# Attention and mixture of experts on one core: the experts' order moved behind the first expert's row numbers, and the low half of w2 taken last in the early tiles

## Chip, cores and metric

The kernel runs on one core of one Trainium2 chip. The metric is the device time of one execution in microseconds (us), as the median over several runs. Engine names are those of the profile: PE is TensorE, PEld its weight loads, DVE is VectorE, ACT is ScalarE, POOL is GpSimd and SP is SyncE.

## What is computed

A linear attention without softmax runs over 8 batches, 8 heads, 576 positions and head dimension 64. Its rows, normalized and scaled, are the 4608 tokens of 512 features of a mixture of 8 experts with one expert per token:

```python
kv = np.einsum('bhsd,bhse->bhde', k, v)
out = np.einsum('bhsd,bhde->bhse', q, kv)
x = out / np.sqrt(np.mean(out * out, axis=-1, keepdims=True) + 1e-06) * g_norm   # as [4608, 512]
...
expert_idx = np.argmax(x @ w_gate, axis=1)         # gate_w: the softmax value of that expert
...                                                # each expert keeps its first 1152 tokens
h = np.maximum(np.einsum('ecd,edf->ecf', disp, w1), 0.0)   # 512 -> 1024
y = np.einsum('ecf,efd->ecd', h, w2)                       # 1024 -> 512
out[i] = gate_w[i] * y[expert_idx[i], pos[i]]
```

## The kernel before

The work has two stages, and each stage's order is written by a planner (class `Plan`). An operation names its engine with an assumed duration, the operations that it depends on, and a key. The planner goes forward in time: of all that is ready it takes what can start first, and the lower key among equals. Each engine then executes its instructions in the order that came out, waiting in order for what is not there yet. A table of small shifts of keys by operation number (`NUDGE`) belongs to each of the two plans.

The first plan runs the attention, batch by batch. `route` finds each token's expert, its place in that expert's list, and enters the token's number into a table in PSUM (`enter`, line 1046), which needs three one-hot products on DVE (`ohh`, `ohl`, `rhs`). It also writes the rows to `x_dram`. Beside it, one expert is chosen early from the tokens of the first batches (`pick`), its two weight matrices are loaded and split into a high and a low half of 16 bits (`high`, `low`, lines 393 to 405), and its first 384 rows go through both products at the end of the plan (`early_products`): three tiles of 128 rows, of which the second product of tile 0 belongs to the first plan and those of tiles 1 and 2 to the second.

Each second product of a tile of 128 rows sums 24 matmuls into one PSUM bank: three blocks of 8, which are the high half of the hidden rows by the high half of w2, the high half by the low half of w2, and the low half of the hidden rows by the high half of w2 (`Gemm2.terms`). The planner issues them in groups of 4 (`second`), and each group depends on those pieces of the hidden rows and of w2 that it reads.

`finish` (line 1343) stands between the stages. It reads the finished table (`read_table`), works out the row numbers of the rest of the first expert's rows (`cut`, whose last instruction writes `gi_rest`, line 1154), the row numbers of all experts (`sources`, line 1145), where results are written (`cut2`, with `targets`), the tokens per expert (`count`, whose result is copied at line 1088), and the order of the other seven experts from that count (`rank_steps`, lines 1108 to 1137: compare, rank, turn and keep, the last of which writes `perm_i`). All of that is on DVE, except for one matmul of the count.

The second plan runs the experts one after the other (`products`). For the first, the remaining 320 rows are gathered by `gi_rest` (POOL, line 457), multiplied by their norm (DVE, line 465), transposed on PE and cast on ACT. For the next expert, POOL copies its number into `next_i` (line 1762) behind those three gathers, SP reads it and starts the loads of w1 (line 345); DVE reads the expert's column of `perm_i` into a register and copies its row numbers (`slots`, lines 668 and 673); POOL gathers its rows, which are transposed by DMA (line 501). Line 713 is a helper of copies and casts, line 551 the first product, line 597 the second, and line 361 the maximum over a piece of weights.

Of the kernel before, what the change touches and what calls it, by code (L numbers as in the profile page):

```python
# [20 lines left out]
EARLY = 384  # L21
# [168 lines left out]
def attention_moe_kernel(  # L190
# [12 lines left out]
    nc = tc.nc  # L203
# [9 lines left out]
    KF = F // P  # L213
# [7 lines left out]
    ep = ctx.enter_context(tc.tile_pool(name="ep", bufs=1))  # L221
# [95 lines left out]
    wsets = [[wts.tile([P, KD * F], F16, name=f"w{n}_0") for n in ("1h", "1l", "2h", "2l")]]  # L317
# [255 lines left out]
    class Gemm2:  # L573


        def __init__(self, pool, ws, g, gt, sidx, s0, s1, bufs=3):
            self.pool, self.g, self.gt, self.sidx, self.s0, self.bufs = pool, g, gt, sidx, s0, bufs
            self.w = [w.rearrange("p (j d) -> p j d", j=KF) for w in ws[2:4]]
            self.tiles = spans(s0, s1)
            self.ysc = pool.tile([P, NHI], F32, name="ysc")  # L580
            hh, hl = g.hh, g.hl
            self.terms = [(h, w, j) for h, w in ((hh, self.w[0]), (hh, self.w[1]), (hl, self.w[0])) for j in range(KF)]

        def scales(self, scale):
            c0 = 0
# [119 lines left out]
    op = plan.op  # L705
# [374 lines left out]
        writes.append(ws)  # L1080
        lasts[b] = ws + [ent, acc]

    def count(dst, key):

        cp = misc[:, 64:64 + E]
        o = op(("T", 0.05), lambda e: nc.tensor.matmul(cp, lhsT=ones16, rhs=tot_acc, start=True, stop=True), accs[-1:], FIRST)
        readers.setdefault("acc", []).append(o)
        return op(("V", 0.1), lambda e: nc.vector.tensor_copy(dst, cp), [o], key)

    def distinct(cnt):  # L1090
        d = sm.tile([P, E], F32, name="dist")
# [72 lines left out]
    early = {}  # L1164
# [97 lines left out]
    def second(r, st, hh, hl, w2, scaled, hid, w_hold, sl_hold, s0, s1, bank, tiles=range(NHI), key=None):  # L1262

        key = KEY * r if key is None else key
        urgent = key - KEY
        for i, (_, m, _) in enumerate(spans(s0, s1)):
            if i not in tiles:
                continue
            yp, o = new(bank[0]), None
            k = key + 5 + 0.1 * i  # L1270
            if m > NARROW:
                for c in range(0, 3 * KF, 4):

                    def product(e, i=i, c=c, yp=yp):
                        if c == 0:
                            yp.t = bank[1]()
                        st["g2"].products(i, yp.t, c, c + 4)

                    js = range(c % KF, c % KF + 4)
                    after = [(hl if c >= 2 * KF else hh)[j] for j in js] + [scaled, o]  # L1280
                    after += [w2[KF <= c < 2 * KF][j] for j in js] if w2 else []
                    o = op(("T", 0.86), product, after, k, (yp,), (hid, w_hold))
            else:
                yt = new("ysb")

                def product(e, i=i, yp=yp):
                    yp.t = bank[1]()
                    st["g2"].turned_products(i, yp.t)

                o = op(("T", 0.1 + TURNED_PAIR[m] if m <= PAIRED else m / 25 + 0.25), product, hh + hl + [scaled] + [x[j] for x in w2 or () for j in range(KF)], k, (yp,),  # L1290
                       (hid, w_hold))
                o = op(("V", 0.07 + (8 if m <= PAIRED else 4) * m / 960), lambda e, i=i, yp=yp: st["g2"].keep(i, yp.t), [o], urgent, (yt,), (yp,))
                yp = new(bank[0])

                def turn(e, i=i, yp=yp):
                    yp.t = bank[1]()
                    st["g2"].turn(i, yp.t)

                o = op(("T", 0.4), turn, [o], key + KEY + 0.05, (yp,), (yt,))
            yh = new("ysb")  # L1300

            def out_(e, i=i, yp=yp, yh=yh):
                yh.t = st["g2"].out(i, yp.t)

            o = op(("A", 0.58), out_, [o], urgent, (yh,), (yp,))
            o = op(("P", 1.05), lambda e, i=i, yh=yh: st["g2"].write(i, yh.t), [o], key, (), (yh, sl_hold))
            o = op(("D", 0.73), None, [o], key, (), (yh,))
        return o

    def early_products():  # L1310
        st = early["st"] = {}
        gates, xh, xl = early["turns"]
        early["hh"], early["hl"] = hh, hl = [], []
        for j in range(KF):
            nm = "x" if j < ON_X else "op"
            hp = new(nm)
            o = None
            for t in range(3):

                def products(e, j=j, t=t, hp=hp, nm=nm):  # L1320
                    if "g1" not in st:
                        st["g1"] = Gemm1(ep, wsets[0], early["x"]().xs, EARLY, EARLY)
                        st["g1"].hidden()
                    hp.t = hp.t or bank(nm)
                    st["g1"].products(j, hp.t, (t,))

                ws = [early["w", 0][t == 2][2 * c + j // (KF // 2)] for c in range(KD)]
                o = op(("T", 4 * EARLY / 2400 + 0.02), products, (xl if t == 1 else xh) + ws + [o], LOW, (hp,))
            a = op(("A", 0.05 + EARLY / 1200), lambda e, j=j, hp=hp: st["g1"].high(j, hp.t), [o], LOW, (), (hp,))
            hh.append(a)  # L1330
            hl.append(op(("V", 0.07 + EARLY / 960), lambda e, j=j, hp=hp: st["g1"].low(j, hp.t), [a], LOW, (), (hp,)))

        def scales(e):
            st["g2"] = Gemm2(ep, wsets[0], st["g1"], early["x"]().gt, early["si"], 0, EARLY, 2)
            st["g2"].scales(y_scale(*[early["z", i]["e"] for i in range(2)]))

        early["scaled"] = op(("V", 1.2), scales, gates + hh[:1] + list(early["w", 1][0].values()), LOW)
        second(-1, st, hh, hl, early["w", 1], early["scaled"], Hold(None), Hold(None), Hold(None), 0, EARLY,
               ("op", lambda: bank("op")), range(EARLY_TILES), LOW + 2)

    cnt_all = cst.tile([P, E], F32, name="cnt_all")

    def finish():
        key = NB * C
        t = op(("V", 0.45), lambda e: read_table(), enters[-1:] + early["slots"] + early["slots2"], key)

        def cut(e):
            early["gi0"] = ep.tile([P, NHI], I32, name="gi_rest")
            sources_of_first(early["gi0"])

        def cut2(e):
            targets()
            early["si0"], = slots(ep, early["first"], ("si",), EARLY)

        early["cut"] = op(("V", 0.65), cut, [t], key)
        early["sources"] = op(("V", 0.2), lambda e: sources(), [t], key + 0.1)
        early["cut2"] = op(("V", 0.8), cut2, [t], key + 0.3)
        o = count(cnt_all, key)
        for long, f in rank_steps(cnt_all):
            o = op(("V", long), lambda e, f=f: f(), [o], key + 0.2)  # L1360
        early["rank"] = o

    tiles = {0: load(0)}
# [446 lines left out]
```

## Time and profile before

| what | us |
|---|---|
| median of 3 runs | 559.38 |
| lowest and highest of them | 556.1 and 563.11 |
| the profiled execution | 556.98 |
| its span, first to last instruction | 555.1 |
| PE busy | 520.3 |
| DVE busy | 394.1 |
| ACT busy | 252.7 |
| POOL busy | 150.9 |

The profiled execution is one run of its own. The span lies 1.9 us under its time, for what stands ahead of the first and behind the last instruction. Its mean granted PE clock is 0.985 of 2.4 GHz. Times within the profile are counted from the first instruction. The attention stage reaches to about 155 us, the experts from there to 548.

### The profile page before, as it was taken

The numbers are of one execution on the slowest core, as the hardware profiler recorded it, in microseconds if no ns is written. First come the engines' busy times: TensorE is split into PE (matmuls) and PEld (weight loads), VectorE is DVE, ScalarE is ACT, GpSimd is POOL, SyncE is SP. The second block draws the span as 40 slices with busy tenths as digits, with TensorE's granted clock in tenths as the row PEclk, the third lists the DMA queues.
The fourth block names the chain that finished last, engine by engine and source line by source line (L and its number), as shares of the span: only waits on it lengthen the run. The fifth ranks groups of instructions, "written<-read, shape, count | busy, mean of one in ns | idle before, by whom it ended". The sixth has DMA issues, their size and how long they took to land.

```text
span 555.1 us, 12017 instructions
## 1 busy us (share of the span) xinstructions
PE 520.3 (94%) x4599; PEld 344.2 (62%) x4599; DVE 394.1 (71%) x1041; ACT 252.7 (46%) x506; POOL 150.9 (27%) x173
## 2 busy tenths in 40 slices
PE   4989797898996999999999999999999999999995
PEld 4878695876544666546754675667468648745442
DVE  3389679989967679869868899779778785751200
ACT  1667475698413346237246282264246165212210
POOL 6001002612356553243404320220503151002011
PEclk9999798899999999999999999999999999999998
DMA  8999999744256979778619538747529341001010
GB/s 272 358 356 360 392 380 368 252 144 182 98 155 249 226 242 264 154 151 266 159 49 322 144 92 280 139 144 259 142 65 305 115 119 38 1 20 58 0 40 32
DMA packets 78019, 102.58 MB, mean 185 GB/s; under 512 B 43222, under 2 KB 51414, under 8 KB 76932
## 3 DMA queue, kind: packets, MB, share of 16 engines
q1 hardware_dynamic: 69600, 70.43, 43.3%
q0 software_dynamic: 7776, 31.30, 16.0%
q8 instruction: 38, 0.62, 0.5%
q14 instruction: 25, 0.20, 0.1%
q10 hardware_dynamic: 580, 0.02, 0.1%
HBM read 73.13 MB, written 20.61 MB: 169 GB/s over the span
## 4 chain that ended last, share of the span: by engine, by line
PE 19%; issue 18%; DMA 11%; DVE 3%; POOL 1%; ACT 1%; POOLq 0%; DVEq 0%
DMA out_dram<-ysb,si 11%; PE hp L551 11%; PE yp L597 6%; DVE am L361 2%; PE yp L612 1%; ACT w2h L395 1%; POOL xg L457 1%; DVE hb L559 1%; POOL out_dram L637 0%; POOL gt L472 0%; POOLq L1740 0%; POOLq L637 0%; DVE xm L465 0%; ACT hb L556 0%; DVE w2l L401 0%
## 5 line engine op out<-in xcount | busy, mean ns | idle before, releaser
L551 PE MATMUL hp<-xs,w1h 128*128 128x320 f16 (+6 forms) x896 | 134.6, 300 | 5.7 <-ACT xs L713 2.6
L597 PEld LDWEIGHTS <-hb 128*128 128x128 f16 x840 | 81.2, 98 | 93.4 <-issue 0.7
L597 PE MATMUL yp<-w2h,hb 128*128 128x512 f16 x544 | 127.1, 379 | 0.3 <-ACT ysb L632 0.2
L551 PEld LDWEIGHTS <-w1h 128*128 128x128 f16 x960 | 93.3, 98 | 46.9 <-issue 7.8
L637 POOL DMA_INDIRECT out_dram<-ysb,si x41 | 46.3, 1130 | 238.1 <-ACT ysb L632 180.8
L361 DVE TENSOR_REDUCE am<-raw 128x1 f32<-128x512 f32 x120 | 75.3, 677 | 12.5 <-DMA raw<-in_moe_w_dram 12.4
L556 ACT ACTIVATE hb<-hp 128x320 f16<-128x320 f32 (+7 forms) x64 | 40.6, 636 | 84.8 <-PE hp L551 70.9
L559 DVE SCALAR_TENSOR_TENSOR hb<-hp,hb 128x320 f16<-128x320 f32 (+7 forms) x64 | 47.2, 737 | 35.8 <-ACT hb L556 35.6
L551 PE MATMUL hp<-xs,w1l 128*128 128x320 f16 (+6 forms) x448 | 71.5, 300 | 0.0
L632 ACT ACTIVATE ysb<-yp,ysc 128x512 f32<-128x512 f32 (+5 forms) x40 | 27.4, 684 | 94.2 <-PE yp L597 90.9
L597 PE MATMUL yp<-w2l,hb 128*128 128x512 f16 x272 | 64.7, 379 | 0.0
L551 PEld LDWEIGHTS <-w1l 128*128 128x128 f16 x480 | 46.9, 98 | 19.4
L457 POOL DMA_INDIRECT xg<-x_dram,gi x35 | 37.1, 1061 | 34.5 <-DVE xm L465 19.8
L861 PE MATMUL op<-kv_bd,qt 128*128 128x144 f32 x256 | 44.2, 316 | 1.6 <-ACT qt L713 1.1
L401 DVE SCALAR_TENSOR_TENSOR w2l<-raw,sw,w2h 128x512 f16<-128x512 f32 x64 | 44.8, 743 | 0.5 <-ACT w2h L395 0.4
L401 DVE SCALAR_TENSOR_TENSOR w1l<-raw,sg,w1h 128x512 f16<-128x512 f32 x64 | 45.0, 746 | 0.0
L491 ACT CAST pair<-xm 128x512 f16<-128x512 f32 (+5 forms) x35 | 21.3, 615 | 46.1 <-DVE xm L465 24.1
L395 ACT ACTIVATE w1h<-raw,sg 128x512 f16<-128x512 f32 x60 | 38.8, 711 | 7.0 <-DVE sg L390 7.0
L395 ACT ACTIVATE w2h<-raw,sw 128x512 f16<-128x512 f32 x62 | 40.1, 713 | 1.0 <-DVE sw L331 1.0
L861 PEld LDWEIGHTS op<-kv_bd,qt 128*128 128x128 f32 x256 | 37.8, 210 | 3.8 <-ACT qt L713 1.8
L772 PE MATMUL a<-v_sb,k_sb 64*64 64x64 f32 x576 | 23.6, 233 | 9.2 <-DMA v_sb<-in_v_dram 7.4
L772 PEld LDWEIGHTS a<-v_sb,k_sb 64*64 64x64 f32 x576 | 20.7, 145 | 12.9 <-issue 11.6
(250 smaller groups left out, 634.6 us busy)
## 6 DMA issues: line engine op xcount, KB each, us to landing
raw<-in_moe_w_dram SPq DMA_DIRECT2D x64, 512.0 KB
k_sb<-in_k_dram SPq DMA_DIRECT2D x16, 576.0 KB
v_sb<-in_v_dram SPq DMA_DIRECT2D x16, 576.0 KB
x_dram<-o_sb POOLq DMA_DIRECT2D x8, 1152.0 KB
q_sb<-in_q_dram SPq DMA_DIRECT2D x16, 512.0 KB
x_dram<-o_sb POOLq DMA_DIRECT2D x8, 144.0 KB
q_sb<-in_q_dram SPq DMA_DIRECT2D x32, 32.0 KB
out_dram<-ysb,si POOLq DMA_INDIRECT x41
```

What stands on the lines that cost most here:

```text
L361: nc.vector.tensor_reduce(out=am()[:, p:p + 1], in_=raw[:, sl(p)], axis=AX.X, op=ALU.max, apply_absolute_value=True)
L395: nc.scalar.activation(wh[:, sl(p)], raw[:, sl(p)], AF.Copy, scale=z["s"])
L401: nc.vector.scalar_tensor_tensor(out=wl[:, sl(p)], in0=raw[:, sl(p)], scalar=z["s"], in1=wh[:, sl(p)], op0=ALU.mult, op1=ALU.subtract)
L457: nc.gpsimd.indirect_dma_start(out=self.xg[i][0:n], out_offset=None, in_=x_dram[0:self.rows, :], in_offset=bass.IndirectOffsetOnAxis(ap=se ...
L551: nc.tensor.matmul(self.view(hp)[:, u], lhsT=w[:, c, j * P:(j + 1) * P], rhs=x[:, c, u * hw:(u + 1) * hw], start=(t == 0 and c == 0), stop ...
L556: nc.scalar.activation(self.out(self.hh, j), self.view(hp), AF.Relu)
L559: nc.vector.scalar_tensor_tensor(out=self.out(self.hl, j), in0=self.view(hp), scalar=0.0, in1=self.out(self.hh, j), op0=ALU.max, op1=ALU.s ...
L597: nc.tensor.matmul(yp[0:n, 0:DM], lhsT=h[:, j, o:o + n], rhs=w[:, j, :], start=(m == 0), stop=(m == len(self.terms) - 1))
L632: nc.scalar.activation(self.ysb[0:n], yp[0:n, 0:DM], AF.Copy, scale=self.ysc[0:n, i:i + 1])
L637: nc.gpsimd.indirect_dma_start(out=out[:, :], out_offset=bass.IndirectOffsetOnAxis(ap=self.sidx[0:n, col:col + 1], axis=0), in_=ysb[0:n], ...
L772: nc.tensor.matmul(banks[g].t[rows[u], half * D:(half + 1) * D], lhsT=kh.t[rows[g], u, c * D:(c + 1) * D], rhs=vh.t[rows[g], u, c * D:(c + ...
L861: nc.tensor.matmul(y, lhsT=qt.t[:, i * P:(i + 1) * P], rhs=kv2[:, half * HH + i], start=True, stop=True)
```

## The change

Two things are changed. In `finish`, the copy of the count and the four pieces of the experts' order get a dependency on `cut`, so the planner can't place them ahead of the first expert's row numbers. In the early tiles (those of the first 384 rows), the second product's three blocks are summed in another order: high by high, low of the hidden rows by high of w2, and then high by low of w2. The dependencies of the groups follow that order. The other tiles keep theirs. Number and form of the instructions, and the numbering of the operations, stay as they were.

```diff
-        def __init__(self, pool, ws, g, gt, sidx, s0, s1, bufs=3):
+        def __init__(self, pool, ws, g, gt, sidx, s0, s1, bufs=3, low_last=False):
...
-            self.terms = [(h, w, j) for h, w in ((hh, self.w[0]), (hh, self.w[1]), (hl, self.w[0])) for j in range(KF)]
+            pairs = [(hh, self.w[0]), (hh, self.w[1]), (hl, self.w[0])]
+            self.terms = [(h, w, j) for h, w in (pairs[::2] + pairs[1:2] if low_last else pairs) for j in range(KF)]
...
-    def count(dst, key):
+    def count(dst, key, behind=None):
...
-        return op(("V", 0.1), lambda e: nc.vector.tensor_copy(dst, cp), [o], key)
+        return op(("V", 0.1), lambda e: nc.vector.tensor_copy(dst, cp), [o, behind], key)
...
-                    after = [(hl if c >= 2 * KF else hh)[j] for j in js] + [scaled, o]
-                    after += [w2[KF <= c < 2 * KF][j] for j in js] if w2 else []
+                    block = (0, 2, 1)[c // KF] if r < 0 else c // KF
+                    after = [(hl if block == 2 else hh)[j] for j in js] + [scaled, o]
+                    after += [w2[block == 1][j] for j in js] if w2 else []
...
-            st["g2"] = Gemm2(ep, wsets[0], st["g1"], early["x"]().gt, early["si"], 0, EARLY, 2)
+            st["g2"] = Gemm2(ep, wsets[0], st["g1"], early["x"]().gt, early["si"], 0, EARLY, 2, True)
...
-        o = count(cnt_all, key)
+        o = count(cnt_all, key, early["cut"])
         for long, f in rank_steps(cnt_all):
-            o = op(("V", long), lambda e, f=f: f(), [o], key + 0.2)
+            o = op(("V", long), lambda e, f=f: f(), [o, early["cut"]], key + 0.2)
```

## Rows read from the trace of the kernel before

**Rows 1.** The page, busy time, share of the span and instructions of each engine

```profile
PE 520.3 (94%) x4599; PEld 344.2 (62%) x4599; DVE 394.1 (71%) x1041; ACT 252.7 (46%) x506; POOL 150.9 (27%) x173
```

**Rows 2.** Windows: length; busy PE, PEld, DVE, ACT, POOL; PEclk; DMA share; GB/s

```profile
94.30:101.10 6.80, 6.50 (x36) 5.72 (x37) 5.91 (x30) 3.93 (x9) 3.91 (x4) 0.50 0.98 371
160.00:170.00 10.00, 7.98 (x43) 3.94 (x41) 4.97 (x13) 1.54 (x3) 7.12 (x9) 1.00 0.84 257
...
180.00:190.00 10.00, 10.00 (x65) 6.05 (x63) 7.01 (x14) 2.88 (x6) 5.62 (x7) 1.00 0.91 225
```

**Rows 3.** Timeline of PE: start, us, line, op, out<-in, count, idle before<-releaser

```profile
91.88 0.71 PE L1046 MATMUL tab<-rhs,ohl 128*128 128x96 f16 x5 [2.49 <-DVE rhs L1039]
...
153.32 1.89 PE L597 MATMUL op<-w2h,hb 128*128 128x512 f16 x8
155.05 0.71 PE L1046 MATMUL tab<-rhs,ohl 128*128 128x96 f16 x5
155.99 3.61 PE L597 MATMUL yp<-w2h,hb 128*128 128x512 f16 x16 [0.23 <-ACT ysb L632]
...
166.94 1.04 PE L597 MATMUL yp<-w2h,hb 128*128 128x512 f16 x4
170.53 2.08 PE L551 MATMUL hp<-xs,w1h 128*128 128x320 f16 x12 [2.56 <-ACT xs L713]
...
174.98 1.25 PE L551 MATMUL hp<-xs,w1h 128*128 128x320 f16 x8 [0.74 <-DVE am L361]
...
177.69 1.25 PE L551 MATMUL hp<-xs,w1h 128*128 128x320 f16 x8 [0.91 <-DVE hb L559]
...
199.69 1.16 PE L551 MATMUL hp<-xs,w1h 128*128 128x336 f16 x7 [0.16 <-DMA xs<-pair]
```

**Rows 4.** Timeline of ACT

```profile
169.62 0.86 ACT L713 CAST xs<-xp 128x512 f16<-128x512 f32 x2 [5.24 <-remote]
```

**Rows 5.** Timeline of POOL

```profile
156.23 1.07 POOL L637 DMA_INDIRECT out_dram<-ysb,si  x1 [5.61 <-DVE tab_sb L1141]
158.15 1.03 POOL L457 DMA_INDIRECT xg<-x_dram,gi_rest  x1 [0.86 <-issue]
...
161.69 0.18 POOL L1762 COPY next_i<-perm_i 1x1 int32<-1x1 int32 x1
...
169.68 1.06 POOL L465 TENSOR_TENSOR xm<-xg 128x512 f32<-128x512 f32 x1 [1.19 <-remote]
```

**Rows 6.** Timeline of DVE, the next expert's w1

```profile
173.25 1.28 DVE L361 TENSOR_REDUCE am<-raw 128x1 f32<-128x512 f32 x2 [0.80 <-DMA raw<-in_moe_w_dram]
```

**Rows 7.** Timeline of DVE around the table and the row numbers

```profile
151.92 0.74 DVE L401 SCALAR_TENSOR_TENSOR w2l<-raw,sw,w2h 128x512 f16<-128x512 f32 x1
...
152.95 0.16 DVE L1088 COPY cnt_all<-misc 128x8 f32<-128x8 f32 x1
...
153.17 0.16 DVE L1092 SCALAR_TENSOR_TENSOR dist<-cnt_all,desc 128x8 f32<-128x8 f32 x1
...
153.71 0.30 DVE L1035 TENSOR_TENSOR ohh<-cols,col 128x240 f16<-128x240 f16 x1
...
154.40 0.45 DVE L1039 TENSOR_TENSOR rhs<-ohh,tok_hl 128x480 f16<-128x480 f16 x1
...
155.80 0.21 DVE L1141 TENSOR_SCALAR tab_sb<-tab 128x48 f32<-128x48 f32 x1
...
156.16 0.16 DVE L1133 CAST perm_i<-perm 128x8 int32<-128x8 f32 x1
...
156.34 0.23 DVE L1150 TENSOR_TENSOR mine<-tab_sb,first 128x48 f32<-128x48 f32 x1
...
156.84 0.44 DVE L1154 TENSOR_SCALAR gi_rest<-mine_g 128x6 int32<-128x6 f32 x1
...
157.92 0.17 DVE L673 COPY gi<-gidx_tab 128x6 int32 x1 [0.58 <-DVE tw L1159]
...
161.70 0.71 DVE L465 TENSOR_TENSOR xm<-xg 128x512 f32<-128x512 f32 x1
```

## The prediction

> **What bounds the kernel now.** I read the page's busy shares first, then the windows of 10 us, then the timelines of the engines around the place of the change. The shares say TensorE: 520.3 of a span of 555.1 us [rows 1]. An average over stages with different limits is not enough, so the windows come next. The change sits at about 150 us, where the attention stage hands over to the expert stage. Ahead of it nothing can move, since the planner places work forward in time and the first changed dependency belongs to work at about 150 us. Behind it the windows show a TensorE that is full: 10.00 of 10 us at 180 to 190 [rows 2], and the same in most windows up to 540. The one exception of size is 160 to 170, with 7.98 of 10 [rows 2]. So a gain can only come from TensorE's idle time from 150 us on, and a loss only from new idle time there.
>
> The timeline of TensorE names those gaps. I count 0.23 us at 155.99, 2.56 at 170.53, 0.74 at 174.98, 0.91 at 177.69 and 0.16 at 199.69 [rows 3], together 4.60 us. That is the most that the change can give back there, 0.8% of the run. Faster by over 2% would take 11 us. I did not use the page's chain of waits: behind its end it runs over the write queue of GpSimd, which TensorE does not wait for.
>
> Who ends the gaps? The first product of the rest of the first expert (170.53) waits for the casts of the transposed rows. ScalarE made two of them from 169.62 on, after 5.24 us of idling, released by something that the profile calls remote [rows 4]. The rows that they cast had been transposed by 166.94 [rows 3], and GpSimd's first norm of the next expert began at 169.68 out of the same kind of wait [rows 5]. So most of the 2.56 us is not the row numbers arriving late; two engines were let go together by one late event. The gap at 174.98 is VectorE's: it held a maximum of the next expert's w1 until the load landed (0.80 us, start 173.25), with the low half that frees the product's bank queued behind it [rows 6].
>
> **Part one: the order behind the row numbers.** It adds no instruction, only moves some on VectorE. Before, the work in front of the first expert's row numbers includes the count's copy (the first of three small instructions between 152.95 and 153.17, so 0.07 us) and the comparison (from 153.17 until 153.71, 0.54 us); both stand ahead of the one-hot products, whose last, rhs, starts at 154.40 and takes 0.45 [rows 7]. Then come three rank pieces, run while TensorE enters the last rows in the table, until the table is read at 155.80 (155.80 - 154.85, some 1.0 us), then the rank's keep (156.16 to 156.34, 0.18 us), and then the cut, whose last instruction writes gi_rest from 156.84 on in 0.44 us [rows 7]. The end is 157.28.
>
> After it, copy, comparison and keep stand behind the cut. The one-hot products come 0.07 + 0.54 = 0.61 us sooner, and the cut another 0.18 sooner. The 1.0 us of rank pieces bring the cut nothing: they were covered by the entering on TensorE. The upper bound is 0.61 + 0.18 = 0.79 us.
>
> The lower bound comes from TensorE's own queue. Entering started at 155.05, straight behind two groups of four products of early tile 0 that ran from 153.32 [rows 3]. With the groups about 0.86 us apart, the boundary between them is at 154.19, and rhs would now end at about 154.24 (154.40 + 0.45 - 0.61). If the plan puts entering between the groups, nearly all of the 0.61 is had; if it leaves it behind both, none is, and 0.18 us remain. I take the middle, 0.5 us, because the boundary and rhs fall within 0.05 us of each other and nothing decides for either side.
>
> What this moves: the first gather (158.15) and the two behind it, then the small copy next_i at 161.69, which GpSimd runs behind the three gathers [rows 5], and which SyncE needs to start the loads of the next expert's w1. All come 0.5 us sooner. The 0.80 us wait for a w1 load then shrinks by 0.5, and with it the 0.74 us gap of TensorE. The gap at 170.53 stays as it is in this sum, by what was said of it.
>
> One thing can eat the move. gi_rest took 0.44 us while GpSimd issued a row write (from 156.23, 1.07 us), and the first instruction of the table's reading, before that write began, took 0.21 [rows 5, 7]; the two engines seem to hold each other up by some 0.2 us an instruction. Behind the change the rank's small instructions run beside the three gathers, where the slot reads did (157.92 to 161.70). If two or three of them hold a gather up by 0.2 us each, the 0.5 us are gone and the sum is zero. I take nothing off, because the gathers ran beside the slot reads already. The Trainium skill has a rule for this, which speaks against the change: SBUF — State Buffer, in its single rule on the shared port pair, has VectorE in a two-port mode and GpSimd, which writes descriptors, exclude each other for a whole instruction. By that rule the sum would be zero too, and the trace's 0.44 us agrees with it in kind.
>
> **What is queued behind the rank now.** The rank ends later: from the cut's end (156.8) come the sources, the targets and the slots of the first expert, about 1.3 us, an estimate: the four slot reads stand (161.70 - 157.92) / 4 = 0.95 us apart, and a few small instructions come beside one [rows 7]. Then come 0.07 + 0.54 + 1.0 + 0.18 = 1.8 us of rank, so its end is at about 159.9. next_i has its turn on GpSimd at 161.2, so 1.3 us of cover stand between; without them the w1 loads would slip by whatever is over. The next expert's slots (gi at 157.92) need the rank too and go to about 160.8 if they follow at once. If the plan puts the first norm of the gathered rows (161.70) ahead of them, they end at about 161.2 + 0.71 + 0.95 = 162.9, while GpSimd could take that expert's first gather at about 161.5. That is a delay of up to 1.3 us for the rows of the next expert, whose products waited for their last transposed rows by 0.16 us already [rows 3]. Their first norm had to wait until 169.68 for another reason [rows 5], so I cost this at nothing; if that wait is gone, up to 1.3 us can show at 199.
>
> **Part two: the low half of w2 last.** The 24 products of an early tile stay 24, of the same shape. In tile 0 the last low-half instruction on VectorE ended at 152.66 (from 151.92, 0.74 us), and the products that follow those of the low half start at 153.32 with no idle time in front of them [rows 3, 7]. So on the chip there was no stall to remove. Tiles 1 and 2 start at 155.99, long behind all halves. Bounds: zero below (no stall seen), and above it the 0.23 us in front of 155.99, which hangs on tile 0's end; I take zero. The wait that it could add is on the low half of the hidden rows, which is ready before the last of w2's.
>
> **The sum.** 0.5 us off the gap at 174.98, zero elsewhere: the profiled execution took 556.98 us, which gives 556.5. The three timed runs have the median 559.38, 2.4 us above the profiled one, and spread over 7 us. Taken from the median, 558.9 us.
>
> **The rivals.**
> *Hidden anyway, no change.* Entering stays behind both groups, or the gathers lose 0.5 us to the small instructions beside them. For it: entering's place is decided by 0.05 us, and the 0.44 us of gi_rest; against it: keep's 0.18 us come in any case. Time 559.4 (559.2 to 559.6).
> *The gap at 170.53 goes as well.* If the remote wait is a chance of that one execution or moves with the gathers, 2.56 us come off beside the 0.5: 556.3. For it: nothing in the kernel explains the wait; against it: it may be in every run of both kernels, or in none of the timed ones of before.
> *Next expert's rows late.* The slots case above: 1.3 us at 199, less 0.5: 560.2.
> *The clock falls (the other side).* A gap of 2.49 us in front of 91.88 [rows 3] was followed by a stretch of 6.80 us at a granted 0.50, that is 1.2 GHz [rows 2], while the 2.56 us gap at 170.53 was not: the clock stayed at 1.00 there [rows 2]. A longer gap or a later one there, from slipped w1 loads, can bring such a stretch in front of full work. Its price is half of 6.80, 3.4 us: 562.8. It decides once the idle time around 168 to 178 grows past what stands there now (2.56, 0.74, 0.91 us); the distance is small since a gap of 2.49 did it elsewhere. The Trainium skill's page TensorE: Matmul & The Clock Gate, Part 1, says the throttled state is the default and activity lifts it. By that rule an idle stretch that grows brings the price again, and the trace agrees with its two levels.
>
> **How the numbers follow.** Forecast (0.2 to 1.0 us faster) 0.36; no change 0.20; the large gap gone 0.20; rows late 0.10; clock 0.10; 0.04 for an order that the plan shifts in a later, now full stage by more than 11 us, 0.03 of it slower. The measurement can tell some 2% (11 us) from no change, so the chances are faster 0.01, same 0.96, slower 0.03. The range takes in the gap gone, less 1.5 us for the spread of runs of one kernel (554.8), up to the clock case (562.8). The likeliest one's own range is 558.4 to 559.2 beside the same median.
>
> **What would show it.** In the changed profile gi_rest should end at about 156.5 to 157.1, the rank's pieces should stand behind it, and next_i at about 161.2. Entering should stand between two groups of four products if the larger gain is had. The maximum of w1 should wait 0.3 us and not 0.80. The forecast is wrong if TensorE is idle in front of 170 for more than 2.6 us, if a second stretch at 0.50 stands behind 150, if the next expert's first product waits for transposed rows by over 1 us, or if a full window behind 180 is full no more.

## The result and the profile after

The changed kernel takes 565.88 us (median of 20 runs, 560.49 to 569.72), against 560.15 for the kernel before beside it (20 runs, 556.1 to 567.15): a ratio of 1.0093, 95% interval [1.0067, 1.0119]. That is within 2%, but it is slower, 3 us over the upper end of the predicted range, where half a microsecond of gain was forecast.

The profiled execution took 566.58 us, with a span of 564.8 against 555.1. The page of the changed kernel, busy time by engine:

```profile
PE 522.7 (93%) x4599; PEld 345.5 (61%) x4599; DVE 396.6 (70%) x1042; ACT 252.9 (45%) x506; POOL 150.8 (27%) x172
```

The work is the same; PE is busy 2.4 us longer [rows 1] and idle 7.3 us longer. Of the 9.7 us, 2.16 were there before the first changed instruction (`hi_i`, ahead of the one-hot products, began at 155.04 against 152.88, on an order of DVE that is the same until then), so they are a difference between two executions. For the rest, windows of the changed kernel (length; busy PE, PEld, DVE, ACT, POOL; granted clock; DMA share; GB/s):

```profile
150.00:200.00 50.00, 45.65 (x319) 26.62 (x318) 40.34 (x113) 16.45 (x31) 26.63 (x28) 1.00 0.66 200
200.00:210.00 10.00, 4.42 (x21) 2.28 (x20) 6.24 (x14) 4.60 (x8) 6.61 (x5) 0.77 0.50 145
210.00:220.00 10.00, 10.00 (x64) 6.49 (x63) 4.96 (x13) 3.29 (x5) 3.32 (x4) 0.89 0.93 354
200.00:250.00 50.00, 44.42 (x264) 26.41 (x263) 35.95 (x69) 18.04 (x29) 21.26 (x24) 0.93 0.68 195
```

And the same two long windows of the kernel before:

```profile
150.00:200.00 50.00, 45.28 (x313) 25.91 (x312) 36.68 (x104) 16.54 (x31) 27.94 (x32) 1.00 0.72 208
200.00:250.00 50.00, 49.49 (x308) 28.87 (x307) 39.55 (x84) 20.32 (x34) 17.66 (x23) 1.00 0.85 210
```

The stretch of the change, 150 to 200, is no worse than before. The loss stands behind it, between 200 and 250, where PE does 5.1 us less, and where the clock fell: a window of 10 us at 0.77 holds 4.6 us at 0.50, that is 1.2 GHz, and one at 0.89 holds 2.2. The timeline of PE in the changed kernel:

```profile
155.48 1.89 PE L598 MATMUL op<-w2l,hb 128*128 128x512 f16 x8
157.21 0.71 PE L1047 MATMUL tab<-rhs,ohl 128*128 128x96 f16 x5
158.15 5.34 PE L598 MATMUL yp<-w2h,hb 128*128 128x512 f16 x24 [0.23 <-ACT ysb L633]
...
172.70 1.25 PE L551 MATMUL hp<-xs,w1h 128*128 128x320 f16 x8 [2.66 <-ACT xs L714]
174.42 0.70 PE L551 MATMUL hp<-xs,w1h 128*128 128x320 f16 x4 [0.47 <-DVE xs L485]
177.74 1.25 PE L551 MATMUL hp<-xs,w1h 128*128 128x320 f16 x8 [0.99 <-DVE p2t L329]
207.56 4.36 PE L551 MATMUL hp<-xs,w1h 128*128 128x336 f16 x15 [5.58 <-DMA xs<-pair]
```

The gaps up to 180 are 0.23, 2.66, 0.47 and 0.99 us, 4.35 together, where they were 4.44 [rows 3]. The new one is 5.58 us at 207.56: the second expert's first products wait for the last of its rows to be transposed. That wait was 0.16 us [rows 3]. Why the rows are late is on POOL and DVE of the changed kernel:

```profile
194.11 1.16 POOL L495 TENSOR_TENSOR pair<-xm,pair 128x512 f16<-128x512 f32 x1 [1.23 <-ACT pair L491]
195.45 3.93 POOL L638 DMA_INDIRECT out_dram<-ysb,si  x1 [0.18 <-ACT w1h L395]
199.38 2.83 POOL L472 COPY gt<-xg 32x1 f32<-32x1 f32 x1
202.18 1.14 POOL L495 TENSOR_TENSOR pair<-xm,pair 32x512 f16<-32x512 f32 x1
```

```profile
194.19 1.63 DVE L465 TENSOR_TENSOR xm<-xg 32x512 f32<-32x512 f32 x1
195.74 2.72 DVE L401 SCALAR_TENSOR_TENSOR w1l<-raw,sg,w1h 128x512 f16<-128x512 f32 x4
...
199.44 2.72 DVE L401 SCALAR_TENSOR_TENSOR w1l<-raw,sg,w1h 128x512 f16<-128x512 f32 x4
```

A row write that takes POOL 1.07 us elsewhere [rows 5] took 3.93, and a copy of 32 numbers 2.83, both beside four low halves of w1 that DVE ran without a break. The last tile's low half (`pair`, 32 rows) stood behind them on POOL, began at 202.18 and ended at 203.32; its transposed rows let PE go on at 207.56. In the kernel before, on POOL:

```profile
193.73 1.03 POOL L637 DMA_INDIRECT out_dram<-ysb,si  x1 [0.18 <-ACT w1h L395]
196.00 1.18 POOL L495 TENSOR_TENSOR pair<-xm,pair 32x512 f16<-32x512 f32 x1 [1.24 <-ACT pair L491]
```

There it ended at 197.18, which is 199.34 with the 2.16 us between the two executions, so some 4.0 of the 5.58 us are its lateness. The rest stands between its end and PE's start, 4.24 us against 2.51 before (199.69 - 197.18); no run here explains that part.

### The profile page after: what moved, and what is told of

Its sections match the earlier page's. It is cut to its first block, busy times and chain, and to the rows that moved or that the text cites. A ratio compares the mean times of both kernels' runs of the same rounds, so it can differ in the third digit from the quotient of the medians.

```text
span 564.8 us, 12013 instructions
## 1 busy us (share of the span) xinstructions
PE 522.7 (93%) x4599; PEld 345.5 (61%) x4599; DVE 396.6 (70%) x1042; ACT 252.9 (45%) x506; POOL 150.8 (27%) x172
## 4 chain that ended last, share of the span: by engine, by line
PE 40%; issue 17%; DMA 11%; DVE 5%; POOL 2%; ACT 1%; POOLq 0%; DVEq 0%; SPq 0%
PE hp L551 20%; PE yp L598 14%; DMA out_dram<-ysb,si 6%; DMA raw<-in_moe_w_dram 3%; PE op L551 2%; PE yp L613 2%; DMA x_dram<-o_sb 1%; DVE w2l L401 1%; PE op L598 1%; DVE am L361 1%; POOL xg L457 1%; POOL gt L472 1%; DMA xs<-pair 1%; ACT w2h L395 1%; DMA xg<-x_dram,gi_rest 1%
## 5 line engine op out<-in xcount | busy, mean ns | idle before, releaser
L551 PE MATMUL hp<-xs,w1h 128*128 128x320 f16 (+6 forms) x896 | 136.1, 303 | 11.6 <-DMA xs<-pair 5.6
L457 POOL DMA_INDIRECT xg<-x_dram,gi x35 | 35.9, 1025 | 45.2 <-DVE am L361 19.1
```

The costliest lines, as they stand in the source:

```text
L457: nc.gpsimd.indirect_dma_start(out=self.xg[i][0:n], out_offset=None, in_=x_dram[0:self.rows, :], in_offset=bass.IndirectOffsetOnAxis(ap=se ...
L551: nc.tensor.matmul(self.view(hp)[:, u], lhsT=w[:, c, j * P:(j + 1) * P], rhs=x[:, c, u * hw:(u + 1) * hw], start=(t == 0 and c == 0), stop ...
```

## The experiments

The plan of the expert stage starts from where the first plan leaves each engine. Printed from the planner, the change moves the early expert's row numbers 0.55 us sooner there and the experts' order 3.5 us later (145.31 to 148.80 us of the plan's time), and with it the time from which DVE is free (146.96 to 148.80). From those times the second plan came out in another order on every engine. Three theories: **A**, that new order costs the time; **B**, the order of the experts is late on the chip and the next expert waits; **C**, the low half taken last costs it. Ratios are to the kernel before in the same runs, with their 95% intervals.

**One part alone, and the order alone.** The first two runs make one part of the change each; the third keeps both parts but starts the second plan from the due times of the kernel before, so that the expert stage has exactly its old order; the fourth is the kernel before with the due times of the changed one.

```diff
-    plan = Plan(plan.free, NUDGE[1])
+    for n, end in {...}.items():
+        plan.ops[n].end = end
+    plan = Plan({...}, NUDGE[1])
```

> Part one alone (the count and the experts' order behind the row numbers), the products' blocks as before. The planner gives the expert stage the same order as in the changed kernel. Theory A (the loss is the expert stage's new order, which follows from the order's later due time): 1.009 times before, some 565 us, with a TensorE gap of 5 to 6 us in front of the second expert's first product. Theory B (the rank is late on the chip itself): the same, 1.009. Theory C (the low half last does it): 1.000, 560 us, no such gap.

Measured: 1.0076 [1.0036, 1.0115]. In its profile PE is busy for 44.58 us between 200 and 250, as in the changed kernel, but the gap of 5 to 6 us in front of the second expert's first product isn't there: the two longest waits are 2.87 us at 221.64 and 2.55 us at 233.57, both for hidden rows. So the loss comes with this order, and the place of the gap doesn't.

> Part two alone (the block with the low half of w2 last), the rank as before. Theory C: 1.009 times before with the gap of 5 to 6 us. Theories A and B: the gap in front of the second expert's first product is not that of the changed kernel. Under A the time is open, since the planner gives the expert stage a third order, and it may be 0.995 to 1.015; under B it is 1.000.

Measured: 1.0142 [1.0094, 1.0189].

> The changed kernel, both parts, but the second plan is started from the due times that the first plan of before ended with, so that the expert stage has exactly the order of before on every engine. The rank still ends some 3 us later on the chip. Theory A: 1.000 times before, 558 to 561 us, second expert's first product waits under 1 us. Theory B: 1.009, some 565 us, the gap stays at 5 us.

Measured: 1.001 [0.9976, 1.0044].

> The kernel before, with neither part of the change, but the second plan is started from the due times of the changed kernel's first plan, so that the expert stage has exactly the changed kernel's order. The rank is early, as before. Theory A: 1.009 times before, some 565 us, with the gap of 5 to 6 us in front of the second expert's first product. Theory B: 1.000, 560 us.

Measured: 1.0101 [1.0051, 1.015]. The change with the old order costs nothing that can be measured, and the kernel before with the new order costs what the change does: theory A holds, and B and C fall. The order that part two alone leads to is a third one, worse than both. The window 200 to 250 of the change with the old order is full again:

```profile
200.00:250.00 50.00, 49.13 (x349) 29.10 (x347) 39.62 (x83) 22.21 (x36) 16.04 (x22) 1.00 0.81 200
```

In the kernel before with the new order, PE did 44.99 of the 50 us, but the gap stands elsewhere. POOL of that run:

```profile
199.09 0.98 POOL L457 DMA_INDIRECT xg<-x_dram,gi  x1 [0.31 <-issue]
200.37 1.02 POOL L637 DMA_INDIRECT out_dram<-ysb,si  x1 [0.30 <-ACT ysb L632]
210.25 1.42 POOL L637 DMA_INDIRECT out_dram<-ysb,si  x1 [8.86 <-DMA out_dram<-ysb,si]
211.98 1.25 POOL L457 DMA_INDIRECT xg<-x_dram,gi  x1 [0.30 <-DVE hb L559]
```

Its DVE and its PE:

```profile
222.06 1.30 DVE L465 TENSOR_TENSOR xm<-xg 128x512 f32<-128x512 f32 x2 [6.29 <-DMA xg<-x_dram,gi]
...
224.47 0.85 DVE L559 SCALAR_TENSOR_TENSOR hb<-hp,hb 128x672 f16<-128x672 f32 x1
```

```profile
225.37 4.51 PE L551 MATMUL hp<-xs,w1h 128*128 128x336 f16 x16 [5.01 <-DVE hb L559]
```

The new order puts two result writes on POOL ahead of the third and fourth row gather of the expert after. POOL idles 8.86 us ahead of the second write, the gathers stand behind it, DVE idles 6.29 us for their rows, and the hidden rows that free PE's bank are queued behind that on DVE: 5.01 us.

**One engine's order at a time.** Each kernel is the changed one whose expert stage is issued from a written list: one set of engines in the order of the kernel before, the others in the new order (line numbers are 6 higher in kernels with a list).

```diff
+        order = self.place()
+        if listed:
+            order = [self.ops[n] for n in listed]
-        for o in self.place():
+        for o in order:
...
-    plan.emit()
+    plan.emit(LISTED)
```

> The changed kernel, with the expert stage's loads and row transposes on SP issued in the order of the kernel before (the second row transpose ahead of the second expert's four w2 loads), and every other engine's order as in the changed kernel. Theory S (the loss is the row transposes queued behind w2 loads): the ratio to before falls from 1.009 to 0.998 to 1.003 and the 5.58 us of PE's wait at 207.56 are gone. Theory V (the order on DVE, ACT and POOL costs it): still 1.007 to 1.012, and the wait stays above 4 us, since the last tile's pair is late whatever SP does. Theory T (the order of the products): still 1.007 to 1.012.

Measured: 1.0352 [1.0304, 1.04].

> The changed kernel, with the expert stage's work on DVE, ACT and POOL in the order of the kernel before, and SP's and PE's as in the changed kernel. Theory V: the ratio to before falls to 0.998 to 1.003. Theory S: still 1.007 to 1.012, with the second expert's first product waiting 4 us or more for a row transpose. Theory T: still 1.007 to 1.012.

Measured: 1.0176 [1.0131, 1.0221].

> The changed kernel, with the expert stage's products on PE in the order of the kernel before, and the other engines' as in the changed kernel. Theory T: the ratio to before falls to 0.998 to 1.003. Theories S and V: 1.007 to 1.012 or more, since the products wait for the same rows and splits.

Measured: 1.0154 [1.0121, 1.0187]. None of the three theories holds: the engine that each of them names brings nothing back, and each mixture is worse than either order whole. Queues that were planned together can't be told apart by swapping one.

**Without the table of nudges.** The second table of key shifts left empty, in the changed kernel and in the one before.

```diff
-    plan = Plan(plan.free, NUDGE[1])
+    plan = Plan(plan.free)
```

> The changed kernel with the second table of NUDGE left empty, so that the plan of the expert stage is made from costs and keys alone. Theory N (what is lost is a fit: the 35 nudges were chosen for the due times of the kernel before, and with others they are worth less): the plan's own last product then ends at 532.5 us, against 530.3 in the changed kernel and 527.8 in the kernel before, so the time is 4 to 8 us over before, ratio 1.007 to 1.015, the changed kernel having kept half of the nudges' worth or less. Rival (the nudges are worth nothing on the chip, and one fault of the new order is the loss): 0.995 to 1.004.

Measured: 1.0047 [1.0023, 1.0072].

> The kernel before with the second table of NUDGE left empty. Theory N (the nudges fit the due times of the kernel before and no others): they are worth to the kernel before what it is faster than the changed kernel without nudges, so this is slower than before by about as much as that one, ratio 1.002 to 1.008, and the change itself then costs nothing. Rival (the nudges do nothing on the chip): 0.998 to 1.002. By the plan's own end of the last product (532.7 us against 527.8) it would be 1.009.

Measured: 1.0158 [1.012, 1.0196]. Both numbers lie outside what either side expected, but the core of theory N shows more strongly than it was put: the same shifts save the kernel before 1.6% and leave the changed kernel 0.5% slower than it is without them (1.0093 against 1.0047). Without them the changed kernel is the faster of the two, 1.0047 against 1.0158. So the sign of the change depends on the order that the planner makes with it.

**Early and late part of the order.** Listed again: one plan's order for all that it starts before 235 us, the other's for the rest (below is the rule that made the list; the kernels have the numbers written out).

```diff
-LISTED = [n for n in new_order]
+LISTED = [n for n in one_order if start[n] < 235] + [n for n in other_order if n not in those]
```

> The changed kernel, whose expert stage issues the first 454 steps of the kernel before's plan (those that start before 235 us in it) in that plan's order, and all steps that are left in the changed plan's order. Theory P (the whole loss is made in the early expert stage, while the second expert's rows are prepared; the order of the later stage is as good): ratio to before 0.997 to 1.004, with PE busy 49 us or more between 200 and 250. Rival (the later order costs as well, as the waits at 320 to 330 and 440 to 450 of the changed kernel say, 1.8 us together): 1.003 to 1.006. Rival (any joint of two orders costs more than either): 1.01 or more.

Measured: 1.006 [1.0034, 1.0087], PE busy 50.00 between 200 and 250.

> The changed kernel, whose expert stage issues the first 440 steps of its own plan (those that start before 235 us in it) in their order, and all steps that are left in the order of the kernel before. Theory P: ratio to before 1.006 to 1.012, PE busy 45 us or less between 200 and 250 and 49 us or more in each 50 us behind it. Rival (the later order is the loss): 0.997 to 1.004.

Measured: 1.0046 [1.0021, 1.0071], PE busy 47.08 between 200 and 250. Theory P ("all of it early") doesn't hold: each mixture costs about half of the loss. Whether that is the part itself or the joint of two orders isn't shown. In the one profile of h5 PE has no wait over 2.51 us behind 150, so it doesn't show where its 0.6% stands.

**The w2 loads.** In the new order the second expert's four w2 loads stand ahead of its second row transpose on SP; in the old one they stand behind it. In h8 and i3 (changed kernel, kernel before) and in i4 (changed kernel, no nudges) they wait in the plan for the third transpose. In i1 only the four loads are moved, in the list of the new order.

```diff
-            sets, zs, w_holds = weights(r + 1, key + 1, before, asked[4:4 + 1] if r == 0 else [])
+            sets, zs, w_holds = weights(r + 1, key + 1, before, asked[4:4 + 1] + sent[2:3] if r == 0 else [])
```

> The changed kernel, in which the second expert's four w2 loads also wait in the plan for the issue of its third row transpose, so that the planner itself puts three row transposes ahead of them on SP (and orders the other engines to suit: four row gathers stand ahead of the out writes on POOL again). The plan's own last product ends at 527.9 us, as the kernel before's 527.8 does. Theory W (of the new order, the loads ahead of the transposes and the out writes ahead of the gathers are what costs): ratio to before 0.996 to 1.003. Rival (the nudges misfire in any plan other than the one they were made for): 1.006 to 1.015.

Measured: 0.9979 [0.9949, 1.0009].

> The kernel before with the same added wait of the second expert's w2 loads for its third row transpose as in the changed kernel's run of it (0.998). If the two parts of the change are worth nothing in themselves: the same ratio, 0.996 to 1.002. If they are worth the 0.5 us that the prediction gave them: up to 0.001 above that one, which the interval can't tell. If the changed kernel's run was luck of one order: anything to 1.015.

Measured: 0.9968 [0.9943, 0.9993].

> The changed kernel with the added wait of the w2 loads for the third row transpose, and the second table of NUDGE empty. The plan's own last product ends at 527.3 us, sooner than the kernel before's 527.8. Theory L or W: with the loads behind three row transposes the tuned nudges aren't needed, ratio 0.994 to 1.002. Rival (without nudges a plan is 0.5 to 1.6 % worse, as in both kernels): 1.003 to 1.016.

Measured: 0.998 [0.9958, 1.0002].

> The changed kernel with every engine's order as it is, but the four loads of the second expert's w2 taken out of SP's order from ahead of its second row transpose and put right behind it; nothing else moves. Theory L (these loads ahead of the transpose make the second expert's first product late): the wait for the last row transpose falls from 5.6 us to 2 us or less and the ratio to before from 1.009 to 0.998 to 1.004. Rival (the order on POOL makes it late: the out writes ahead of the last tile's copy and pair): the wait stays above 4 us, ratio 1.007 to 1.012. Rival (a foreign order on one engine costs more than it brings, as SP's whole order of before did): 1.012 or more.

Measured: 1.0088 [1.006, 1.0117]; in its profile the wait for the transpose is 0.9 us, and one of 4.86 us for hidden rows stands at 232.90 instead. The added wait mends the changed kernel, but not by the loads' place: moved alone, they leave the loss where it was. What the wait also did is to bring the planner to another order, in which all four gathers stand ahead of both writes (h8, i3) or of the second (i4).

**The two writes.** In i2 the two writes on POOL are moved behind the fourth gather in the list of the new order, nothing else. In j1 the third and fourth gather of the kernel before are moved behind the two writes. j2 is the kernel before with the order of i2. The steps on POOL in i2 (97 and 103 are the writes, the others the gathers):

```diff
-    322, 330, 97, 103, 338, 346,
+    322, 330, 338, 346, 97, 103,
```

> The changed kernel with every engine's order as it is, but the two out writes on POOL that stand ahead of the third and fourth row gathers of the next expert put right behind the fourth; nothing else moves. Theory G (the writes ahead of the gathers keep POOL from the last tile's copy and pair, and the gathers late): the wait at 207.56 falls to 2 us or less and the one at 225 (5.0 us in the kernel before with the new order) doesn't appear, ratio 0.998 to 1.004. Theory L: 1.006 to 1.012, with the wait for the row transpose above 4 us.

Measured: 0.9947 [0.992, 0.9974], below what theory G expected and the lowest ratio of all, though its interval overlaps those of i3, h8 and i4. Its POOL and its window:

```profile
194.41 0.19 POOL L478 COPY gt<-xg 32x1 f32<-32x1 f32 x1
...
200.96 0.96 POOL L463 DMA_INDIRECT xg<-x_dram,gi  x1 [0.31 <-issue]
202.22 1.44 POOL L463 DMA_INDIRECT xg<-x_dram,gi  x1 [0.30 <-issue]
203.97 1.09 POOL L644 DMA_INDIRECT out_dram<-ysb,si  x1 [0.30 <-issue]
213.22 1.15 POOL L644 DMA_INDIRECT out_dram<-ysb,si  x1 [8.16 <-DVE pair L501]
```

```profile
200.00:250.00 50.00, 49.88 (x300) 29.04 (x300) 41.81 (x86) 24.25 (x39) 18.38 (x24) 1.00 0.78 224
```

The last write still waits 8.16 us, now with the four gathers ahead of it. The two late gathers start at 200.96 and 202.22, and PE is full. Two of 1,570 steps moved take the changed kernel from 1.0093 to below the kernel before.

> The kernel before with one move on POOL: the third and fourth row gathers of the second next expert stand behind the two out writes of the first expert instead of ahead of them, which is their place in the changed kernel; every other order is that of before. Theory G (a gather behind an out write waits for that write's result tile, some 8 us, and the expert's rows are late): 1.005 to 1.015, PE losing 4 us or more between 200 and 250, in a wait for a maker of hidden rows or transposed rows behind 215. Rival (the move is harmless in an order that is otherwise the old one): 0.998 to 1.003.

Measured: 1.0025 [0.9995, 1.0055]. The rival holds in the timed runs: the same place of the writes in the old order costs little or nothing. Its profiled execution, the slowest of its 12 (563.79 against a median of 558.36), does show the predicted wait, after 7.56 us of POOL before the second write:

```profile
234.37 1.23 PE L603 MATMUL yp<-w2h,hb 128*128 128x512 f16 x2 [4.52 <-ACT hb L562]
```

> The kernel before with the changed kernel's order of the expert stage in which the two out writes are moved behind the gathers (the order of i2, 0.9947). If the mended order is the gain and the two parts of the change are worth nothing on the chip: 0.992 to 0.998 as i2. If the parts are worth the 0.5 us of the prediction, it is 0.001 above i2, which the intervals can't tell apart. If the gain needs the sooner row numbers of the change: 0.999 to 1.004.

Measured: 1.0007 [0.9964, 1.005]. That speaks for the third case, that the gain of i2 needs the change as well, but its interval still meets that of i2. Five of its twelve times lie between 553.46 and 555.80 us and seven between 559.98 and 562.00, with none in between, so 1.0007 lies between two outcomes. The profiled one (560.86) belongs to the seven. It shows the other gap, the one of the changed kernel at 207.56, though its writes are in the good place. POOL and PE of j2:

```profile
191.11 3.92 POOL L643 DMA_INDIRECT out_dram<-ysb,si  x1 [0.18 <-ACT w1h L401]
195.04 2.79 POOL L478 COPY gt<-xg 32x1 f32<-32x1 f32 x1
```

```profile
203.21 4.17 PE L557 MATMUL hp<-xs,w1h 128*128 128x336 f16 x15 [5.61 <-DMA xs<-pair]
```

And of h6, which has the new order there too:

```profile
190.75 3.93 POOL L644 DMA_INDIRECT out_dram<-ysb,si  x1 [0.18 <-issue]
194.68 2.90 POOL L478 COPY gt<-xg 32x1 f32<-32x1 f32 x1
```

```profile
202.92 3.40 PE L557 MATMUL hp<-xs,w1h 128*128 128x336 f16 x12 [5.54 <-DMA xs<-pair]
```

So the new order has two weak places on POOL. One is the writes ahead of the gathers (5.01 us in e4, 4.86 in i1). The other is the early write and copy ahead of the last tile's pair, when they fall beside DVE's run of low halves (5.58 us in the changed kernel, 5.54 in h6, 5.61 in j2). Each of these profiles shows one or the other. That fits, since products that lose 5 us for the pair need the gathers' rows 5 us later, but it isn't shown. i2 mends the first by its order, and its profile is free of the second. Nothing that i2 moves stands ahead of the early write and copy, so that second part isn't shown to come from its edit.

Which of the two a profile shows isn't set by the order: the changed kernel, e1 and e4 have one order on every engine. POOL and DVE of e4, ahead of the same place:

```profile
191.89 1.72 POOL L495 TENSOR_TENSOR pair<-xm,pair 128x512 f16<-128x512 f32 x1 [1.26 <-ACT pair L491]
193.79 1.28 POOL L637 DMA_INDIRECT out_dram<-ysb,si  x1 [0.18 <-ACT w1h L395]
195.07 0.45 POOL L472 COPY gt<-xg 32x1 f32<-32x1 f32 x1
```

```profile
191.92 0.67 DVE L465 TENSOR_TENSOR xm<-xg 32x512 f32<-32x512 f32 x1
193.15 3.00 DVE L401 SCALAR_TENSOR_TENSOR w1l<-raw,sg,w1h 128x512 f16<-128x512 f32 x4 [0.56 <-ACT w1h L395]
```

DVE's multiplication of 32 rows by their norm (`xm`) takes 0.67 us here, POOL's `pair` beside it takes 1.72, DVE then waits 0.56 us for ACT, and the write and the copy get through beside the four low halves in 1.28 and 0.45 us. In the changed kernel `pair` took 1.16 and the multiplication 1.63, the low halves followed it without a wait, and the write and the copy were long. h6 and j2 are like the changed kernel (multiplication 1.53 and 1.66 us); e1, i1 and i2 are like e4 (0.67 each). In the changed kernel and in e4, `pair` and the multiplication begin within 0.08 us of each other, so one order can go either way there. How often each happens in the timed runs isn't known; j2's two groups of times would fit it.

**The plan's own end.** The due end of the plan's last product, beside what was measured, for the kernels whose order the planner made:

| kernel | plan's last product | ratio |
|---|---|---|
| i4 | 527.3 | 0.998 |
| i3 | 527.7 | 0.9968 |
| before, e3 | 527.8 | 1, 1.001 |
| h8 | 527.9 | 0.9979 |
| changed, e4 | 530.3 | 1.0093, 1.0101 |
| e1 | 530.4 | 1.0076 |
| h4 | 532.5 | 1.0047 |
| h7 | 532.7 | 1.0158 |
| e2 | 535.1 | 1.0142 |

These are eight different orders, since e1 has the order of the changed kernel. Every plan that ends at 527.9 or sooner is as fast as before or a little faster, and every plan that ends 2.5 us later than before's or more is slower. The size isn't given by it (h4 is off by half), the sign is.

## Why the prediction was wrong

- **The step that failed** is the one that reckoned what is queued behind the rank. It followed the moved instructions over the chip (gather, `next_i`, slots) as if the expert stage were then issued in its old order, and the sum took "zero elsewhere". It is issued from a plan that starts where the first plan's engines come free, and part one's due times moved that plan (e1; whether by the rank's 3.5 us or by the row numbers' 0.55 wasn't tried), though the moved instructions themselves cost nothing on the chip (e3). The new order had 0.04 of the chance, and only with a loss of over 11 us. e3 (1.001) and e4 (1.0101) show that it is the whole loss, some 5 us.
- **The bound was right:** "a loss only from new idle time" behind 150. So were the marks set for a wrong forecast: a full window behind 180 that is full no more (44.42 of 50), rows waited for by over 1 us (5.58), a second stretch at half clock. The fourth mark, idle time in front of 170 of over 2.6 us, was passed by its letter alone: 2.66 where it was 2.56.
- **Part one** gave about its least. Entering stayed behind both groups of products (155.48, then 157.21 on PE). DVE of the changed kernel:

```profile
155.04 0.16 DVE L1024 TENSOR_SCALAR hi_i<-pos_all 128x5 int32<-128x5 int32 x1
...
156.18 0.46 DVE L1040 TENSOR_TENSOR rhs<-ohh,tok_hl 128x480 f16<-128x480 f16 x1
157.96 0.21 DVE L1142 TENSOR_SCALAR tab_sb<-tab 128x48 f32<-128x48 f32 x1 [1.32 <-PE tab L1047]
...
158.95 0.17 DVE L1155 TENSOR_SCALAR gi_rest<-mine_g 128x6 int32<-128x6 f32 x1
...
161.85 0.17 DVE L1135 TENSOR_SCALAR perm_i<-perm 128x8 int32<-128x8 f32 x1
163.08 0.17 DVE L674 COPY gi<-gidx_tab 128x6 int32 x1 [1.06 <-issue]
```

  DVE now idles 1.32 us for the table. `gi_rest` begins 3.91 us behind `hi_i`, where it was 3.96 (156.84 - 152.88 [rows 7]), so 0.05 us were had, not 0.5; its end gains 0.3, since it took 0.17 and not 0.44. A row write on POOL ran beside it again (158.39, 1.06 us), so the 0.44 wasn't that write's doing alone, and the hold-up of 0.2 us an instruction that the prediction read from it didn't return at this place. "Nothing decides for either side" was fair, but the middle of two outcomes is neither: the likelier one was to be taken.
- **The rank's cover held.** `perm_i` ended at 162.0 and `next_i` had its turn at 163.56, behind the three gathers; 1.5 us of cover against 1.3 estimated. Less the 2.16 us these are 159.9 and 161.4, where 159.9 and 161.2 were reckoned. POOL of the changed kernel:

```profile
158.39 1.06 POOL L638 DMA_INDIRECT out_dram<-ysb,si  x1 [5.61 <-DVE tab_sb L1142]
...
163.56 0.71 POOL L1764 COPY next_i<-perm_i 1x1 int32<-1x1 int32 x1
```

  The slots came late as said (163.08) and cost nothing: with the old order (e3) the second expert's first product waits 0.34 us.
- **Part two** costs nothing on the chip, as taken (e3 has both parts); alone it leads the planner to the order with the latest end, 535.1 (1.0142).
- **The rivals.** "Next expert's rows late" named the place, by the wrong road and at a quarter of the price. "The clock falls" came true, but in the new gap and not around 168 to 178: some 6.8 us at 1.2 GHz from 205.5 on, of which 2.1 were idle, so the other 4.7 cost some 2.4 us, against the 3.4 priced for work that fills the whole stretch. "The gap at 170.53 goes" didn't: ACT waited for a remote release again, 4.60 us until 171.78.

## What to carry to other kernels

Where a planner writes the order, a changed dependency is costed twice: once by what its instructions do on the chip, and once by what its due times do to everything that is planned behind it. The plan's own end told the sign in all eight orders here, and hand-made shifts that fit one set of due times can be worth 1.6% there and cost 0.5% with another. When a new order loses, look on each in-order queue for an instruction that waits long with gathers or loads behind it: moving two writes was worth 1.5% in this order, though nothing that could be measured in the old one.

## What the runs showed of the hardware

- In the changed kernel, h6 and j2 a row write and a small copy on POOL lasted as long as DVE's run of low halves, not one of them: 3.93, 3.93 and 3.92 us for the write, 2.83, 2.90 and 2.79 for the copy, where i2 has 1.03 and 0.19. Each time DVE ran four low halves in 2.72 us; the write ended some 0.9 us behind its run, the copy within 0.05 us of the end of the next one. The Trainium skill, SBUF — State Buffer, under "Who interferes with whom", has a DVE instruction with two inputs in SBUF contend with a POOL instruction that reads SBUF; these three copies agree with it. But in e4 and e1 the same write and copy beside four low halves took 1.28 and 1.27, 0.45 and 0.46 us, and the four low halves 3.00 us; and in e4 two gathers on POOL, at 197.48 and 199.09, took 1.30 and 0.98 us beside four low halves in 2.72 us, so what lets POOL in between is open, as is how often the timed runs meet it. The planner marks the low halves and the pairs as users of a common port, the write and the copy not.
- The wait for a remote release ahead of the first expert's rest is in the changed kernel as in the one before (2.66 and 2.56 us of PE), and not in e3, where three other waits (1.52, 0.87 and 1.91 us) take its place. Its cause wasn't found.
- Still open: where the 0.6% of h5 stands, and why the writes' place is worth 1.5% in the new order and hardly anything in the old one.
